# A WKV recurrence with routed experts on one core: block rows transposed on VectorE, strip sums on VectorE, two wide logits, one transfer for keys and decays

## The chip, the cores and the metric

One Trainium2 chip, one core of it, one launch. The metric is the device time of the program in microseconds (us); lower is better. All arithmetic that decides the result is float32.

## The reference

```python
def _attn_ref(r, k, v, w, u):                 # (4, 8, 768, 48) each, u (8, 48)
    for t in range(S):
        cur = einsum('bhd,bhe->bhde', u[None] * kt, vt)
        y[:, :, t] = einsum('bhd,bhde->bhe', rt, state + cur)
        state = wt[:, :, :, None] * state + einsum('bhd,bhe->bhde', kt, vt)

def _moe_ref(x, modality_id, w_gate, modality_bias, w1, w2):   # x (3072, 384)
    logits = x @ w_gate + modality_bias[modality_id]           # 8 experts
    e_idx = argmax(logits, axis=1)
    gate_w = softmax(logits)[arange(N), e_idx]
    for e in range(E):
        mask = e_idx == e
        h = maximum(x[mask] @ w1[e], 0.0)                      # 384 -> 1024
        out[mask] = gate_w[mask, None] * (h @ w2[e])           # 1024 -> 384
```

The rows of x are the attention's outputs with the heads side by side. Each row goes to one expert, its best.

## The kernel before, in words

The program has two stages. In the first, 24 units of 128 time steps (6 chunks in each of 4 sequences) run through a chunked form of the recurrence (`att_iter`). The loop is software-pipelined: in iteration `i` the decays and keys of unit `i+3`, the scan of unit `i+2`, the scores of unit `i+1` and the output of unit `i` are worked on. A unit's inputs are three parts of one tile of 1536 columns: r (0 to 512), k (512 to 1024) and the decays (1024 to 1536). `load` issues them on SP's queue, here in three transfers for units 4 to 23 (L913). The output of a unit (L455, PSUM tile `pY`) is added up into a row tile `xp` by VectorE (`x_rows`, L477). TensorE then transposes these rows, and `logits` (L504) multiplies them with the gate's weights, in six matmuls with 64 output rows each. Rows, gate weights and row numbers are scattered by expert into a table `xs` in HBM, one indirect transfer of GpSimd per unit (L711).

In the second stage seven blocks of rows run through an expert each: two of 512 rows, three of 384, one of 512, one of 416 (`WIDTH`; numbered 0 to 6 here). For block `q`:

- `blk_load(q)` (L732) brings its rows from `xs` into the tile `xl`, in one transfer on SP's queue, rows on partitions. It is issued one or more blocks ahead; block 0's is issued in iteration 20 of the first stage, block 1's waits for the scatters of the first ten units.
- `blk_t(q)` (L745) turns the rows: TensorE transposes them 64 rows at a time into four PSUM areas (L755; L758 for the odd 32 rows of block 6), ScalarE casts them to `xh` (L765), and VectorE takes the remainder to `xo` (L767). For block 0 this stands in the last iteration of the first stage, for block 2 ahead of the last tile of block 1's second half, for the others right behind the first half of the block before.
- `blk_up(q, g)` for g from 0 to 7 (L778) is the first half: nine matmuls each of 384 to 512 columns, with the weights split in two parts `wh` and `wl`. ScalarE evicts (`hh`, L782), VectorE takes the remainder (`hl`, L783).
- `blk_down(q, fs, js)` (L799) is the second half, one tile `j` of 128 rows after the other into `pY` and `pX` in turn, 24 matmuls each. `blk_out` (L817) scales it on ScalarE (`ot`, L822) and writes it with an indirect transfer of GpSimd (L823).
- The 32 odd rows of block 6 are a strip of their own: `strip_down` (L802) gives four partial sums on four groups of 32 partitions, ScalarE copies them (L810), and `strip_sum` (L813) adds them with a matmul against the matrix `fold`.

Between these calls the program runs small steps from a table `aux` (which block, which half, which step): the splitting of the next expert's weights (`w_split`, L270: a cast on ScalarE, a remainder on VectorE), the routing table, the scatters of later units, weight loads. Each engine carries out its instructions in the order of the program.

Of the kernel before, what the change touches and what calls it, by code (L numbers as in the profile page):

```python
# [70 lines left out]
def kernel(ctx: ExitStack, tc: tile.TileContext, rkw, vt, wf, cst, mid, wg, bias, w1, w2, out):  # L71
# [238 lines left out]
    def ok(n):  # L310
        return 0 <= n < NU
# [35 lines left out]
    def att_iter(i):  # L347
# [384 lines left out]
    def blk_load(q, at=None):  # L732
        at = q if at is None else at
        w = width(q) // P
        rest = width(q) % P
        xl = bp["m"].tile([P, BW // P, XW], F32, tag="xl", name=f"xl{q}", bufs=3)
        r = nc.sync.value_load(tab[0:1, 1, ds(at, 1)], min_val=0, max_val=DUMMY)
        ins = nc.sync.dma_start(out=xl[:, 0:w], in_=xs[ds(r, w * P), :].rearrange("(j p) c -> p j c", p=P))
        if q == 0:
            tc.add_to_no_dep_group("x0", ins.ins)  # L740
        if rest:
            nc.sync.dma_start(out=xl[0:rest, w], in_=xs[ds(r + w * P, rest), :])
        X["xl", q] = xl

    def blk_t(q):  # L745
        xl, w = X["xl", q], width(q)
        xh, xo = (bp["m"].tile([P, KC, BW], F32R, tag=t, name=f"{t}{q}", bufs=1) for t in ("xh", "xo"))
        pk, pu, nj = pt(f"x{q}_0", "pK", (P, 2, 512)), pt(f"x{q}_2", "pU"), w // P
        halves, m = [(0, KC - 1, (pk[:, 0], pk[:, 1])), (KC - 1, KC, (pu, pt(f"x{q}_3", "pS1" if q == WB else "pX")))], w % P
        for c0, c1, pp in halves:  # L750
            for c in range(c0, c1):
                for j in range(nj):
                    for pb, r in zip(pp, HALVES):
                        o = ((c - c0) * nj + j) * 64
                        nc.tensor.transpose(out=pb[:, o:o + 64], in_=xl[r, j, c * P:(c + 1) * P], identity=ident[r, r])  # L755
        o = 64 * nj
        for c in range(KC if m else 0):
            nc.tensor.transpose(out=pu[:, o + c * m:o + (c + 1) * m], in_=xl[0:m, nj, c * P:(c + 1) * P], identity=ident[0:m, 0:m])  # L758
        view = lambda t, c0, c1, h: t[:, c0:c1, 0:nj * P].rearrange("p c (j h b) -> p c j h b", h=2, b=64)[:, :, :, h]
        moves = [(lambda t, c0=c0, c1=c1, h=h: view(t, c0, c1, h), pb[:, 0:(c1 - c0) * nj * 64].rearrange("p (c j b) -> p c j b", c=c1 - c0, j=nj))  # L760
                 for c0, c1, pp in halves for h, pb in enumerate(pp)]
        if m:
            moves.append((lambda t: t[:, :, nj * P:w], pu[:, o:o + KC * m].rearrange("p (c b) -> p c b", c=KC)))
# [4 lines left out]
        X["x", q] = (xh, xo)  # L768

# [32 lines left out]
    def strip_down(q, j):  # L802
        r0, r1 = spans(width(q))[j]
        pp = pt(f"d{q}_{j}", "pK", (P, DM))
        for f in range(FC):
            i = f % (P // TAIL) * TAIL
            nc.tensor.matmul(out=pp[i:i + TAIL], lhsT=X["ht", q][:, f], rhs=raw[1][:, f],
                             start=(f < P // TAIL), stop=(f + P // TAIL >= FC), skip_group_check=True)
        st = bp["p"].tile([P, GW], F32, tag="wg", name=f"st{q}", bufs=2)[:, 0:DM]
        nc.scalar.copy(out=st, in_=pp)  # L810
        X["st", q] = st

    def strip_sum(q, j):  # L813
        X["y", q, j] = pt(f"s{q}_{j}", "pU", (P, DM))
        nc.tensor.matmul(out=X["y", q, j][0:TAIL], lhsT=fold, rhs=X["st", q], start=True, stop=True)

    def blk_out(q, js):  # L817
        xl = X["xl", q]
        for j in js:
            m = min(P, width(q) - j * P)  # L820
            ot = bp["p"].tile([P, DM], F32, tag="ot", name=f"ot{q}_{j}", bufs=4)
            nc.scalar.activation(out=ot[0:m], in_=X["y", q, j][0:m], func=AF.Copy, scale=xl[0:m, j, DM:DM + 1])  # L822
            ins = nc.gpsimd.indirect_dma_start(  # L823
                out=out[:, :], out_offset=bass.IndirectOffsetOnAxis(ap=xl[0:m, j, DM + 1:DM + 2].bitcast(I32), axis=0),
                in_=ot[0:m], in_offset=None, bounds_check=NT - 1, oob_is_err=False)
            if isinstance(q, int):
                rows_apart("out", ins)


    def half_load(q, at=None):  # L830
        at = q if at is None else at
        xl = bp["m"].tile([P, BW // P, XW], F32, tag="xl", name=f"xl{q}", bufs=3)
        r = nc.sync.value_load(tab[0:1, 1, ds(at, 1)], min_val=0, max_val=DUMMY)
        nc.sync.dma_start(out=xl[:, 0], in_=xs[ds(r, P), :])
        X["xl", q] = xl

    def half_t(q):
        pp = pt(f"x{q}", tag="pK", sh=(P, KC, P))
        for c in range(KC):
            nc.tensor.transpose(out=pp[:, c], in_=X["xl", q][:, 0, c * P:(c + 1) * P], identity=ident)  # L840
        X["x", q] = bp["p"].tile([P, KC, P], F32, tag="xq", name=f"xq{q}", bufs=1)
        nc.scalar.copy(out=X["x", q], in_=pp)
# [49 lines left out]
    for i in range(-2, NU):  # L892
# [93 lines left out]
    at(q1, "u", 6, part(nc.vector.tensor_reduce, out=fold, in_=ident.rearrange("p (i r) -> p r i", r=TAIL), axis=AX.X, op=ALU.add))  # L986
    fl = flags()
# [3 lines left out]
    for n, q in enumerate(seq):  # L991
# [10 lines left out]
        for j in range(nj):  # L1002
# [14 lines left out]
            if nxt is None and j == 1:  # L1017
                strip_sum(q, nj)
                blk_out(q, (nj,))
# [39 lines left out]
    def any_decay():  # L1059
# [40 lines left out]
        with tc.tile_pool(name="gmoe", bufs=1) as gp:  # L1100
# [48 lines left out]
def _layout(inp):  # L1149
# [15 lines left out]
    for hh in range(2):  # L1165
# [40 lines left out]
```

## Time and profile before

| what | value |
|---|---|
| median of 3 runs | 347.0 us (344.35 to 347.06) |
| profiled execution, own time | 345.26 us |
| its span, first to last instruction | 343.1 us |
| TensorE busy (matmul) | 329.9 us, 96% |
| VectorE, ScalarE, GpSimd busy | 225.7, 205.9, 156.4 us |
| granted TensorE clock, mean | 0.998 |

The span is 2.2 us shorter than the execution's own time. Matmul ends are modelled, so the busy share of TensorE is not its share of peak; the starts of its instructions are what the text reads. The first stage lasts to about 121 us of the span, the second from there to the end.

### The profile page before, as it was taken

The numbers are of one execution on the slowest core, as the hardware profiler recorded it, in microseconds if no ns is written. First come the engines' busy times: TensorE is split into PE (matmuls) and PEld (weight loads), VectorE is DVE, ScalarE is ACT, GpSimd is POOL, SyncE is SP. The second block draws the span as 40 slices with busy tenths as digits, with TensorE's granted clock in tenths as the row PEclk, the third lists the DMA queues.
The fourth block names the chain that finished last, engine by engine and source line by source line (L and its number), as shares of the span: only waits on it lengthen the run. The fifth ranks groups of instructions, "written<-read, shape, count | busy, mean of one in ns | idle before, by whom it ended". The sixth has DMA issues, their size and how long they took to land.

```text
span 343.1 us, 10458 instructions
## 1 busy us (share of the span) xinstructions
PE 329.9 (96%) x4064; PEld 303.2 (88%) x4064; DVE 225.7 (66%) x495; ACT 205.9 (60%) x524; POOL 156.4 (46%) x194
## 2 busy tenths in 40 slices
PE   7989999999999999999999999999999999999992
PEld 3788899989989987799889999999999988999972
DVE  7999999999999565871578369468067055615500
ACT  2577588687799874632467459658658645514320
POOL 5889999999996383075542201200200200121022
PEclk9999999999999999999999999999999999999999
DMA  7998988888983302248728300700700812210001
GB/s 230 400 288 244 293 272 262 272 254 243 313 249 111 94 3 97 90 151 255 247 88 249 121 2 0 254 23 0 278 24 3 303 36 91 107 50 18 1 26 59
DMA packets 24672, 52.32 MB, mean 153 GB/s; under 512 B 3045, under 2 KB 11045, under 8 KB 24612
## 3 DMA queue, kind: packets, MB, share of 16 engines
q1 hardware_dynamic: 21508, 42.08, 38.8%
q0 software_dynamic: 3104, 9.47, 7.5%
q8 instruction: 34, 0.56, 0.7%
q14 instruction: 26, 0.21, 0.2%
HBM read 55.43 MB, written 11.88 MB: 196 GB/s over the span
## 4 chain that ended last, share of the span: by engine, by line
issue 45%; PE 24%; POOL 12%; DMA 8%; DVE 3%; ACT 3%; POOLq 2%; SPq 0%; ACTq 0%
POOL out L823 6%; PE pY L455 5%; DMA in<-rkw 5%; PE pS L411 4%; POOL xs L711 4%; PE pY L444 4%; PE pR_x L317 3%; PE pU L429 2%; PE pR_x L507 2%; DMA xl<-xs 1%; POOLq L1016 1%; DMA v<-vt 1%; POOL wl L273 1%; PE pY_d L799 1%; ACT dV L352 1%
## 5 line engine op out<-in xcount | busy, mean ns | idle before, releaser
L823 POOL DMA_INDIRECT out<-ot,xl x25 | 26.1, 1046 | 141.2 <-ACT ot L822 139.9
L783 DVE SCALAR_TENSOR_TENSOR hl<-pS_u,hh 128x512 fp32r<-128x512 f32 (+2 forms) x56 | 34.6, 619 | 74.4 <-ACT hh L782 74.2
L778 PE MATMUL pS_u<-xh,wh 128*128 128x512 f32 (+2 forms) x168 | 61.8, 368 | 0.0
L778 PE MATMUL pS_u<-xh,wl 128*128 128x512 f32 (+2 forms) x168 | 61.3, 365 | 0.0
L782 ACT ACTIVATE hh<-pS_u 128x512 fp32r<-128x512 f32 (+2 forms) x56 | 30.3, 541 | 51.6 <-PE pS_u L778 51.5
L273 DVE TENSOR_TENSOR wl<-raw,wh 128x768 fp32r<-128x768 f32 x52 | 48.8, 963 | 3.6 <-ACT wh L272 3.3
L272 ACT CAST wh<-raw 128x768 fp32r<-128x768 f32 (+1 forms) x60 | 45.1, 799 | 0.0
L778 PE MATMUL pS_u<-xo,wh 128*128 128x512 f32 (+2 forms) x168 | 43.2, 365 | 0.0
L799 PE MATMUL pY_d<-wh,hh 128*128 128x384 f32 x112 | 38.5, 343 | 0.0
L799 PE MATMUL pY_d<-wl,hh 128*128 128x384 f32 x112 | 37.7, 337 | 0.0
L799 PE MATMUL pY_d<-wh,hl 128*128 128x384 f32 x112 | 37.7, 336 | 0.0
L711 POOL DMA_INDIRECT xs<-xp,posT x24 | 26.0, 1083 | 24.9 <-DVE posT L594 22.2
L331 DVE TENSOR_TENSOR_SCAN pX_s<-pw,pX_s 128x268 f32<-128x268 f32 x48 | 34.1, 710 | 0.8 <-POOL pw L278 0.4
L778 PEld LDWEIGHTS pS_u<-xh,wh 128*128 128x128 f32 x168 | 31.5, 188 | 3.2
L778 PEld LDWEIGHTS pS_u<-xh,wl 128*128 128x128 f32 x168 | 31.5, 188 | 3.1
L778 PEld LDWEIGHTS pS_u<-xo,wh 128*128 128x128 f32 x168 | 31.0, 188 | 3.4
L283 POOL TENSOR_TENSOR G<-in 128x512 f32<-128x512 f32 x24 | 31.4, 1310 | 4.3 <-DMA in<-rkw 4.3
L352 ACT ACTIVATE dV<-v,dT 128x48 f32<-128x48 f32 x120 | 29.7, 327 | 0.0
L413 DVE TENSOR_TENSOR A<-pS,cs 128x1024 f32<-128x1024 f32 x24 | 29.2, 1217 | 0.6 <-PE pS L411 0.6
L411 PE MATMUL pS<-R,K 64*128 64x128 f32 x384 | 27.0, 280 | 1.9 <-DVE A L413 1.4
L295 POOL TENSOR_TENSOR in<-in 128x512 f32<-128x512 f32 (+1 forms) x23 | 28.5, 1239 | 0.6
L455 PE MATMUL pY<-v,A 128*64 128x48 f32 x768 | 26.8, 222 | 0.7 <-issue 0.7
(331 smaller groups left out, 674.9 us busy)
## 6 DMA issues: line engine op xcount, KB each, us to landing
raw<-w SPq DMA_DIRECT2D x24, 768.0 KB
in<-rkw SPq DMA_DIRECT2D x66, 256.0 KB
v<-vt SPq DMA_DIRECT2D x24, 192.0 KB
wg<-wf SPq DMA_DIRECT2D x8, 576.0 KB
raw<-w SPq DMA_DIRECT2D x8, 384.0 KB
xl<-xs SPq DMA_DIRECT2D x3, 772.0 KB
xl<-xs SPq DMA_DIRECT2D x4, 579.0 KB
xs<-zt SPq DMA_DIRECT2D x8, 193.0 KB
```

Of the source, the lines that this page charges most:

```text
L272: nc.scalar.copy(out=wh[k][:, sl], in_=raw[k][:, sl])
L273: (eng or (nc.vector, nc.gpsimd)[k]).tensor_tensor(out=wl[k][:, sl], in0=raw[k][:, sl], in1=wh[k][:, sl].bitcast(F32), op=ALU.subtract)
L283: nc.gpsimd.tensor_tensor(out=G, in0=t[:, 0:512], in1=t[:, 512:1024], op=ALU.mult)
L331: nc.vector.tensor_tensor_scan(out=BE[:, ::step], data0=pp[:, ::step], data1=d1[:, ::step], initial=0.0, op0=ALU.mult, op1=ALU.max)
L352: nc.scalar.activation(out=dV[:, h], in_=v0[:, h], func=AF.Copy, scale=dT[:, h:h + 1])
L411: nc.tensor.matmul(out=pS[:, hh, p], lhsT=K[q, p], rhs=R[q, p], start=True, stop=True)
L455: nc.tensor.matmul(out=pY[q:q + 64, h * D:(h + 1) * D], lhsT=A[:, hh, p, q:q + 64], rhs=v[:, h * D:(h + 1) * D], start=(first(z) and h == ...
L711: rows_apart("xs", nc.gpsimd.indirect_dma_start(out=xs[:, :], out_offset=bass.IndirectOffsetOnAxis(ap=posT[:, n:n + 1], axis=0), in_=T["xb ...
L778: nc.tensor.matmul(out=pp, lhsT=wsrc[0][:, g, c * P:(c + 1) * P], rhs=xsrc[:, c, 0:w], start=(n == 0), stop=(n == 3 * KC - 1))
L783: nc.vector.scalar_tensor_tensor(out=hl, in0=pp, scalar=0.0, in1=hh.bitcast(F32), op0=ALU.max, op1=ALU.subtract)
L799: nc.tensor.matmul(out=X["y", q, j][0:r1 - r0], lhsT=hsrc[:, r0:r1], rhs=wsrc[1][:, f], start=(f == 0 and n == 0), stop=(f == FC - 1 and n ...
L823: ins = nc.gpsimd.indirect_dma_start(out=out[:, :], out_offset=bass.IndirectOffsetOnAxis(ap=xl[0:m, j, DM + 1:DM + 2].bitcast(I32), axis=0 ...
```

## The change

1. `blk_load` brings a block's rows in four transfers of 96 columns each, every one to 32 partitions (tile `xq`), and a fifth for gate weight and row number (tile `xg`). VectorE transposes squares of 32 by 32 (`blk_turn`, three instructions to a block) into an SBUF tile `xt`, from which ScalarE casts `xh` and VectorE takes `xo`, three instructions each. The rows of `w1` are stored in the order that this gives. No matmul of TensorE is left in `blk_t`. For block 0 two of the three turns stand behind iteration 22 and one behind the row sum of iteration 23.
2. The strip's four partial sums are added by one copy of 32 partitions on ScalarE and three additions on VectorE; the matmul with `fold` is gone.
3. The logits of units 22 and 23 are three matmuls of 128 output rows instead of six of 64.
4. Keys and decays of units 4 to 23 come in one transfer of 1024 columns.

```diff
         if ok(z - 1) and not far(z - 1):
             x_rows(z - 1)
+        if i == NU - 1:
+            blk_turn(0, (2,))
...
             nc.scalar.copy(out=T["xT", z - 2], in_=pS.rearrange("p h (a b) -> p h a b", a=KC))
-            blk_t(0)
+            blk_parts(0)
...
+        if i == NU - 2:
+            blk_turn(0, (0, 1))
...
     def logits(n):
+        if n >= NU - 2:
+            for c in range(KC):
+                nc.tensor.matmul(out=T["R"][:, n * E:(n + 1) * E], lhsT=T["xT", n][:, c], rhs=wgs[:, c],
+                                 start=(c == 0), stop=(c == KC - 1), skip_group_check=True)
+            return
...
     def blk_load(q, at=None):
...
-        xl = bp["m"].tile([P, BW // P, XW], F32, tag="xl", name=f"xl{q}", bufs=3)
-        ins = nc.sync.dma_start(out=xl[:, 0:w], in_=xs[ds(r, w * P), :].rearrange("(j p) c -> p j c", p=P))
+        xq, xg = x_tiles(q)
+        ins = [nc.sync.dma_start(out=xq[SQ * g:SQ * g + SQ, 0:w // SQ],
+                                 in_=xs[ds(r, w), QW * g:QW * g + QW].rearrange("(t p) c -> p t c", p=SQ)) for g in range(4)]
+        ins.append(nc.sync.dma_start(out=xg[:, 0:nj], in_=xs[ds(r, nj * P), DM:XW].rearrange("(j p) c -> p j c", p=P)))
...
+    def blk_turn(q, cs):
+        w = width(q)
+        if 0 in cs:
+            X["xt", q] = bp["m"].tile([P, KC, BW], F32, tag="xt", name=f"xt{q}", bufs=1)
+        for c in cs:
+            nc.vector.transpose(out=X["xt", q][:, c, 0:w], in_=X["xq", q][:, 0:w // SQ, SQ * c:SQ * c + SQ])
+
+    def blk_parts(q):
+        xt, w = X["xt", q], width(q)
+        xh, xo = X["x", q] = tuple(bp["m"].tile([P, KC, BW], F32R, tag=t, name=f"{t}{q}", bufs=1) for t in ("xh", "xo"))
+        for c in range(KC):
+            nc.scalar.copy(out=xh[:, c, 0:w], in_=xt[:, c, 0:w])
+        for c in range(KC):
+            nc.vector.tensor_tensor(out=xo[:, c, 0:w], in0=xt[:, c, 0:w], in1=xh[:, c, 0:w].bitcast(F32), op=ALU.subtract)
...
     def blk_t(q):
-                        nc.tensor.transpose(out=pb[:, o:o + 64], in_=xl[r, j, c * P:(c + 1) * P], identity=ident[r, r])
...
-            nc.tensor.transpose(out=pu[:, o + c * m:o + (c + 1) * m], in_=xl[0:m, nj, c * P:(c + 1) * P], identity=ident[0:m, 0:m])
...
-        for at, pp in moves:
-            nc.scalar.copy(out=at(xh), in_=pp)
-        for at, pp in moves:
-            nc.vector.tensor_tensor(out=at(xo), in0=pp, in1=at(xh).bitcast(F32), op=ALU.subtract)
+        blk_turn(q, range(KC))
+        blk_parts(q)
...
-        nc.scalar.copy(out=st, in_=pp)
-        X["st", q] = st
-
-    def strip_sum(q, j):
-        X["y", q, j] = pt(f"s{q}_{j}", "pU", (P, DM))
-        nc.tensor.matmul(out=X["y", q, j][0:TAIL], lhsT=fold, rhs=X["st", q], start=True, stop=True)
+        nc.scalar.copy(out=st, in_=pp[0:TAIL])
+        for i in range(TAIL, P, TAIL):
+            nc.vector.tensor_tensor(out=st, in0=pp[i:i + TAIL], in1=st, op=ALU.add)
+        X["y", q, j] = st
...
-            load(i + 2 + NIN, ((512, 1024), (1024, LIN), (0, 512)))
+            load(i + 2 + NIN, ((512, LIN), (0, 512)))
```

Three places of the order. First VectorE at the end of the first stage: `A` is the score mask of unit 23, `xp` the row sum of unit 22, `xt` the turned rows of block 0, `hl_0` its first remainder. Before:

```order
L413 TENSOR_TENSOR A_2692<-pS_2693,cs 128x1024
L477 TENSOR_TENSOR xp_1450<-pY_2717,dV_2680 128x384
L767 TENSOR_TENSOR xo_2768<-pK_x_0_2769,xh_2767 128x8x64 x2
L767 TENSOR_TENSOR xo_2768<-pU_x_2_2770,xh_2767 128x4x64
L767 TENSOR_TENSOR xo_2768<-pX_x_3_2771,xh_2767 128x4x64
L783 SCALAR_TENSOR_TENSOR hl_0_2898<-pS_u_0_2887,hh_0_2897 128x512
```

And in the changed kernel:

```order
L417 TENSOR_TENSOR A_2677<-pS_2678,cs 128x1024
L768 STREAM_TRANSPOSE xt_2735<-xq_2549 128x512 x2
L483 TENSOR_TENSOR xp_1437<-pY_2702,dV_2665 128x384
L768 STREAM_TRANSPOSE xt_2735<-xq_2549 128x512
L776 TENSOR_TENSOR xo_2757<-xt_2735,xh_2756 128x512 x3
L795 SCALAR_TENSOR_TENSOR hl_0_2857<-pS_u_0_2846,hh_0_2856 128x512
```

Two turns now stand ahead of the row sum of unit 22, so that sum waits in VectorE's queue for block 0's load.

Second ScalarE behind block 0's first half: `hh_7` is that half's last eviction, `xh` block 1's rows, `ex` the exponential of the routing, `wh` the next weights, `ot_0` and `ot_1` block 0's first results. Before:

```order
L782 ACTIVATE hh_7_3060<-pS_u_7_3050 128x512
L765 CAST xh_3072<-pK_x_0_3074 128x8x64 x2
L765 CAST xh_3072<-pU_x_2_3075 128x4x64
L765 CAST xh_3072<-pX_x_3_3076 128x4x64
L567 ACTIVATE ex<-pR_x 128x14x8
L272 CAST wh_68<-raw_66 128x768 x2
L822 ACTIVATE ot_0_3167<-pY_d_0_3109,xl_2569 128x384
L272 CAST wh_68<-raw_66 128x768 x2
L822 ACTIVATE ot_1_3239<-pX_d_1_3172,xl_2569 128x384
```

And in the changed kernel:

```order
L794 ACTIVATE hh_7_3018<-pS_u_7_3008 128x512
L774 CAST xh_3034<-xt_3030 128x512 x3
L578 ACTIVATE ex<-pR_x 128x14x8
L274 CAST wh_68<-raw_66 128x768 x2
L832 ACTIVATE ot_0_3100<-pY_d_0_3042,xg_2550 128x384
L274 CAST wh_68<-raw_66 128x768 x2
L832 ACTIVATE ot_1_3172<-pX_d_1_3105,xg_2550 128x384
```

The casts stand where they stood; they now read what VectorE has turned, and the first result is still queued behind them.

Third ScalarE at the end of the last block, with the strip (`st`, tile 3 of that block) between the results of its tiles 0, 1 and 2. In the changed kernel:

```order
L832 ACTIVATE ot_0_5096<-pY_d_0_5070,xg_4520 128x384
L822 COPY st_5110<-pK_d_3_5101 32x384
L832 ACTIVATE ot_3_5140<-st_5110,xg_4520 32x384
L832 ACTIVATE ot_1_5145<-pX_d_1_5115,xg_4520 128x384
L832 ACTIVATE ot_2_5175<-pY_d_2_5150,xg_4520 128x384
```

The order of ScalarE's steps is as before, with an `st` of 32 partitions instead of 128; what left is the matmul on TensorE between the tiles 1 and 2.

## Rows read from the trace of the kernel before

**Rows 1.** The page: busy time, share and instructions of each engine.

```profile
PE 329.9 (96%) x4064; PEld 303.2 (88%) x4064; DVE 225.7 (66%) x495; ACT 205.9 (60%) x524; POOL 156.4 (46%) x194
```

**Rows 2.** Timeline of TensorE (start, length, line) around the transposes of blocks 2, 5, 6.

```profile
188.65 0.34 PE L799 MATMUL pY_d<-wl,hh 128*128 128x384 f32 x1
188.82 0.33 PE L799 MATMUL pY_d<-wh,hl 128*128 128x384 f32 x1
...
190.07 0.33 PE L799 MATMUL pX_d<-wl,hh 128*128 128x384 f32 x1
...
258.81 0.69 PE L778 MATMUL pS_u<-xo,wh 128*128 128x384 f32 x3
...
260.62 0.36 PE L799 MATMUL pY_d<-wl,hh 128*128 128x384 f32 x1
...
289.05 0.86 PE L778 MATMUL pS_u<-xo,wh 128*128 128x512 f32 x3
...
291.13 0.34 PE L799 MATMUL pY_d<-wl,hh 128*128 128x384 f32 x1
```

**Rows 3.** Timeline of TensorE around the transposes of block 1.

```profile
139.25 0.39 PE L778 MATMUL pS_u<-xh,wl 128*128 128x512 f32 x1
139.48 0.86 PE L778 MATMUL pS_u<-xo,wh 128*128 128x512 f32 x3
140.95 0.71 PE L755 MATMUL pK_x<-cs,xl 64*128 64x64 f32 x16 [0.61 <-DMA xl<-xs]
...
142.12 0.34 PE L799 MATMUL pY_d<-wl,hh 128*128 128x384 f32 x1
```

**Rows 4.** Timeline of ScalarE behind block 0's first half, and one row of VectorE.

```profile
143.19 0.31 ACT L567 ACTIVATE ex<-pR_x 128x112 f32<-128x112 f32 x1
143.34 1.60 ACT L272 CAST wh<-raw 128x768 fp32r<-128x768 f32 x2
...
147.10 0.58 ACT L822 ACTIVATE ot<-pY_d,xl 128x384 f32<-128x384 f32 x1 [2.16 <-PE pY_d L799]
...
142.55 0.28 DVE L561 TENSOR_REDUCE ohs<-oh 128x8 bf16<-128x80 bf16 x1
```

**Rows 5.** Timeline at the end of the first stage: VectorE, then TensorE.

```profile
118.38 0.56 DVE L477 TENSOR_TENSOR xp<-pY,dV 128x384 f32<-128x384 f32 x1 [1.42 <-ACT wh L272]
...
119.25 0.88 PE L444 MATMUL pY<-SPb,R 128*64 128x96 f32 x16
```

**Rows 6.** Block 0's load on SP's queue, and block 1's in the chain.

```profile
110.65 0.40 SPq L738 DMA_DIRECT2D xl<-xs  x1
...
135.95 4.96 DMA xl<-xs
```

**Rows 7.** DMA views of 3.0:3.5, 3.5:4.0 and 18.0:18.5; q1: packets, MB, share.

```profile
q1 hardware_dynamic: 102, 0.20, 102.8%
...
DMA packets 195, 0.15 MB, mean 307 GB/s; under 512 B 30, under 2 KB 150, under 8 KB 195
...
q1 hardware_dynamic: 195, 0.15, 95.8%
...
DMA packets 244, 0.16 MB, mean 329 GB/s; under 512 B 147, under 2 KB 209, under 8 KB 244
...
q1 hardware_dynamic: 244, 0.16, 112.2%
```

**Rows 8.** The page's groups: form, count, busy, mean ns of one, idle before.

```profile
L783 DVE SCALAR_TENSOR_TENSOR hl<-pS_u,hh 128x512 fp32r<-128x512 f32 (+2 forms) x56 | 34.6, 619 | 74.4 <-ACT hh L782 74.2
L413 DVE TENSOR_TENSOR A<-pS,cs 128x1024 f32<-128x1024 f32 x24 | 29.2, 1217 | 0.6 <-PE pS L411 0.6
```

**Rows 9.** Timeline of the last block: TensorE around the strip's sum, then GpSimd.

```profile
331.53 0.33 PE L799 MATMUL pX_d<-wh,hl 128*128 128x384 f32 x1
...
332.83 0.33 PE L799 MATMUL pY_d<-wl,hh 128*128 128x384 f32 x1
...
337.92 0.98 POOL L823 DMA_INDIRECT out<-ot,xl  x1 [2.22 <-ACT ot L822]
```

More of the change, by code (lines that the diff above doesn't have):

```diff
@@ L36 @@
 BT = WIDTH[-1]
+SQ = 32
+QW = DM // 4
 TAIL = BT % P
@@ L733, in blk_load @@
         at = q if at is None else at
-        w = width(q) // P
-        rest = width(q) % P
-        xl = bp["m"].tile([P, BW // P, XW], F32, tag="xl", name=f"xl{q}", bufs=3)
+        w = width(q)
+        nj, rest = divmod(w, P)
+        xq, xg = x_tiles(q)
         r = nc.sync.value_load(tab[0:1, 1, ds(at, 1)], min_val=0, max_val=DUMMY)
-        ins = nc.sync.dma_start(out=xl[:, 0:w], in_=xs[ds(r, w * P), :].rearrange("(j p) c -> p j c", p=P))
+        ins = [nc.sync.dma_start(out=xq[SQ * g:SQ * g + SQ, 0:w // SQ],
+                                 in_=xs[ds(r, w), QW * g:QW * g + QW].rearrange("(t p) c -> p t c", p=SQ)) for g in range(4)]
@@ L739, in blk_load @@
+        ins.append(nc.sync.dma_start(out=xg[:, 0:nj], in_=xs[ds(r, nj * P), DM:XW].rearrange("(j p) c -> p j c", p=P)))
         if q == 0:
-            tc.add_to_no_dep_group("x0", ins.ins)
+            for i in ins:
+                tc.add_to_no_dep_group("x0", i.ins)
         if rest:
-            nc.sync.dma_start(out=xl[0:rest, w], in_=xs[ds(r + w * P, rest), :])
-        X["xl", q] = xl
-    def blk_t(q):
[L746 to L754, printed above, removed]
-                        nc.tensor.transpose(out=pb[:, o:o + 64], in_=xl[r, j, c * P:(c + 1) * P], identity=ident[r, r])
-        o = 64 * nj
-        for c in range(KC if m else 0):
-            nc.tensor.transpose(out=pu[:, o + c * m:o + (c + 1) * m], in_=xl[0:m, nj, c * P:(c + 1) * P], identity=ident[0:m, 0:m])
[L759 to L763, printed above, removed]
-        for at, pp in moves:
-            nc.scalar.copy(out=at(xh), in_=pp)
-        for at, pp in moves:
-            nc.vector.tensor_tensor(out=at(xo), in0=pp, in1=at(xh).bitcast(F32), op=ALU.subtract)
-        X["x", q] = (xh, xo)
@@ new lines, in blk_load, with x_tiles @@
+            nc.sync.dma_start(out=xg[0:rest, nj], in_=xs[ds(r + nj * P, rest), DM:XW])
+    def x_tiles(q):
+        xq = X["xq", q] = bp["m"].tile([P, BW // SQ, QW], F32, tag="xq", name=f"xq{q}", bufs=2)
+        xg = X["xg", q] = bp["m"].tile([P, BW // P, 2], F32, tag="xg", name=f"xg{q}", bufs=3)
+        return xq, xg
+    def blk_turn(q, cs):
+        w = width(q)
+        if 0 in cs:
+            X["xt", q] = bp["m"].tile([P, KC, BW], F32, tag="xt", name=f"xt{q}", bufs=1)
+        for c in cs:
+            nc.vector.transpose(out=X["xt", q][:, c, 0:w], in_=X["xq", q][:, 0:w // SQ, SQ * c:SQ * c + SQ])
@@ L831, in half_load @@
         at = q if at is None else at
-        xl = bp["m"].tile([P, BW // P, XW], F32, tag="xl", name=f"xl{q}", bufs=3)
+        xq, xg = x_tiles(q)
         r = nc.sync.value_load(tab[0:1, 1, ds(at, 1)], min_val=0, max_val=DUMMY)
-        nc.sync.dma_start(out=xl[:, 0], in_=xs[ds(r, P), :])
-        X["xl", q] = xl
+        for c in range(KC):
+            nc.sync.dma_start(out=xq.rearrange("p t c -> p (t c)")[:, c * P:(c + 1) * P].rearrange("p (g i) -> p g i", i=SQ),
+                              in_=xs[ds(r, P), 0:DM].rearrange("p (g k i) -> p g k i", g=4, k=KC)[:, :, c])
+        nc.sync.dma_start(out=xg[:, 0], in_=xs[ds(r, P), DM:XW])
     def half_t(q):
@@ L839, in half_t @@
         for c in range(KC):
-            nc.tensor.transpose(out=pp[:, c], in_=X["xl", q][:, 0, c * P:(c + 1) * P], identity=ident)
+            nc.tensor.transpose(out=pp[:, c], in_=X["xq", q].rearrange("p t c -> p (t c)")[:, c * P:(c + 1) * P], identity=ident)
         X["x", q] = bp["p"].tile([P, KC, P], F32, tag="xq", name=f"xq{q}", bufs=1)
@@ L1017 @@
             if nxt is None and j == 1:
-                strip_sum(q, nj)
                 blk_out(q, (nj,))
@@ L1104, in any_decay @@
             wgf = mk("gwg", [P, KC, E])
-            nc.sync.dma_start(out=wgf, in_=wg.rearrange("(c p) e -> p c e", p=P))
+            for g in range(4):
+                nc.sync.dma_start(out=wgf[SQ * g:SQ * g + SQ], in_=wg[QW * g:QW * g + QW].rearrange("(c i) e -> i c e", i=SQ))
             with tc.For_i(0, E, 1) as e:
@@ L1110, in any_decay @@
                 with tc.For_i(0, NU, 1) as n:
-                    nc.sync.dma_start(out=xl, in_=xd[ds(n * P, P), :])
+                    for c in range(KC):
+                        nc.sync.dma_start(out=xl[:, c * P:(c + 1) * P].rearrange("p (g i) -> p g i", i=SQ),
+                                          in_=xd[ds(n * P, P), :].rearrange("p (g k i) -> p g k i", g=4, k=KC)[:, :, c])
                     px, pl, ph, py = pt("gx", "pX"), pt("gl", "pR"), pt("gh", "pS0"), pt("gy", "pY")
```

17 lines of the change are left out of this document (7 added, 10 removed).

## The prediction

> **What bounds the kernel now.** I read the page first. TensorE is busy 96% of the span, the next engine 66% [rows 1], and the granted clock is full throughout, so nothing is to be had from the clock. Then I followed TensorE's own timeline through the second stage, by the starts of its instructions, because the ends are modelled. Inside a half the starts are evenly spaced: 0.17 us for a matmul of 384 columns [rows 2], 0.23 us for one of 512 [rows 3]. TensorE is only off this beat where something else stands in its queue: at each block's transposes and at the strip's sum. So in this stage a microsecond taken out of TensorE's queue is a microsecond off the end, as long as what stood beside it is not late. The end confirms this: the last result goes out when GpSimd has waited 2.22 us for ScalarE [rows 9], which follows the last matmul.
>
> There is one true wait of TensorE in the stage: 0.61 us at block 1, for the load of its rows [rows 3]. The loads of blocks 0 and 1 are the two that are issued late, since they wait for scatters; those of the others are issued most of a block ahead. So I looked at the loads next (SP's timeline, the chain, the DMA view), because the change makes them slower.
>
> **The transposes of blocks 2 to 6 (the main gain).** The cost of a block's transposes is the distance between the last matmul ahead and the second one behind, less the beats that belong to matmuls. I take the second one because the first still loads its weights behind the transposes.
> - Block 2, 18 transposes: 190.07 - 188.82 = 1.25, less two beats of 0.17: 0.91 us. Blocks 3 and 4 have the same 18, so 3 x 0.91 = 2.73.
> - Block 5, 24 of them: 260.62 - 258.81 = 1.81, less four beats of 0.17: 1.13.
> - Block 6, 18 and 3 of the odd rows: 291.13 - 289.05 = 2.08, less three beats of 0.23 and one of 0.17: 1.22 [rows 2, 3].
> Together 5.1 us. In their place VectorE gets three turns per block. None is in the trace. The nearest row is `hl` with as many columns, 0.62 us; the other end is 1.22 us, what VectorE takes for 1024 columns [rows 8]. I take 0.62, since the form is one pass over 512 columns; it can't be nothing, each being an instruction of full width. The casts and remainders stay and become three of each. What hides them is the second half of the block before, 12.5 us for three tiles. Tightest is ScalarE's queue: casts of `xh`, four of `wh`, then the first result, which must be out before the third tile can use the same PSUM area, 48 beats or 8.4 us behind the start. At 0.62 a turn this leaves over a microsecond. For block 2 the turns come later, ahead of the last tile, and their cover is that tile.
>
> **Block 1.** Distance 142.12 - 139.48 = 2.64, less three beats of 0.23 and one of 0.17: 1.78 us, the wait for the load included [rows 3]. Not all comes home. The routing matmuls behind the first twelve matmuls need `ohs`, which VectorE ends at 142.83 [rows 4]; without the transposes TensorE is there at 140.17 + 2.1 = 142.3. So 0.5 us turn into a new wait, and 1.28 remain, if the load isn't too late (below).
>
> **Block 0.** Its transposes end where TensorE starts L444, at 119.25. That matmul overwrites `pY`, so it needs the row sum of unit 22, which VectorE ends at 118.94 [rows 5]. Of the transposes only 0.25 us can be gained; the rest becomes a wait for that sum. Two turns now stand ahead of that sum. VectorE was idle for 1.42 us there, from 116.96 [rows 5]; two turns of 0.62 are done at 118.2 and just fit. At 1.22 each they end at 119.4 and L444 starts at 120.0: a loss of 0.8.
>
> **The load in small packets.** One transfer of 512 packets of 1.5 KB becomes four of 512 packets of 384 bytes: 128 to each of the 16 DMA engines instead of 32. From 3.0 to 3.5 us nearly all packets have 2 KB: 102.8% of 16 x 0.5 us over 102 packets is 81 ns each. From 3.5 to 4.0 us, 45 of these leave 4.0 us for 150 smaller ones, most of 512 bytes: 27 ns each. From 18.0 to 18.5 us, 35 of 2 KB and 62 between leave 147 under 512 bytes with 16 to 30 ns, depending on what the 62 cost (61 or 27 ns) [rows 7]. I take p = 27 ns for 384 bytes; the ends are 16 and, if a packet costs the same whatever its size, 81. Block 1's load took 4.96 us [rows 6], of which 32 packets of 61 ns (by size from 81) are 1.95; the fixed part is 3.0. The issues of the four transfers, 0.4 us each [rows 6], run beside the data. So a load lands 3.0 + 0.128 p (p in ns) behind its first issue: 6.5 us.
> - Block 0: 110.65 + 6.5 = 117.1, some 0.15 behind VectorE's idle start. With turns, sum and hand-over (1.24 + 0.56 + 0.05) L444 starts at 119.0 at the earliest. Net: 3.74 - 0.128 p, at most 0.25.
> - Block 1: 135.95 + 6.5 = 142.4. ScalarE then needs three turns (1.86), the last cast (0.6), the exponential (0.31), two casts of weights (1.60) and the result (0.58) [rows 4]: 147.4. TensorE needs the PSUM area at 140.17 + 8.4 + 0.5 = 149.1. Cover is 1.7 us, gone from p = 40 ns; beyond it costs 0.128 ns for ns.
>
> The Trainium skill (DMA: Bandwidth & Descriptors, section Specifications) sets 512 bytes as the smallest transfer at line rate, with a read-modify-write below. The rows of 18.0 to 18.5 us don't show that: packets under 512 bytes cost no more there than those of 512 [rows 7]. By the rule p would be higher than 27; what that does is the third rival.
>
> For the turn the skill has a price (VectorE: DVE Perf Modes, the three transpose paths): 311 ns for 128 by 128 in bf16. Four of these, as an estimate, are 1.24 us, the upper end above. No trace here shows it; by it the sum would be that of the second rival.
>
> **The strip.** 332.83 - 331.53 = 1.30, less two beats: 0.96 us off TensorE's queue, with 5.3 us of work still to come behind it [rows 9]. VectorE's three additions (under 0.6 each by the rows of VectorE) run beside tile 1 and have nothing behind them. Since the strip's own result goes out earlier, GpSimd is free for the last one.
>
> **Logits and merged load.** The two wide logits have half the matmuls with twice the weight columns: I count nothing, with 0.3 us either way. The merged transfer carries the same bytes to a unit that is used two iterations later; decays came second before and land with the keys now. At 81 ns per 2 KB, 128 packets more on 16 engines are 0.65 us, once, if an early unit waits; an issue of 0.4 us on SP's queue is the most that it can save there. Later GpSimd and TensorE set the pace, so zero.
>
> **Sum.** 5.1 + 1.28 + 0.25 + 0.96 = 7.6 us. From the profiled execution's 345.26 that gives 337.7; from the median of the runs, 347.0, it gives 339.4. I forecast the middle, 338.5 (base 346.1).
>
> **Rivals.**
> 1. The freed time is eaten by a wait that takes its place: the first result of a block, behind turns, casts and weights on ScalarE, holds the third tile. For it: that queue order [rows 4] and a gap of a microsecond only. Against: by the rows it fits in every block. Then only the strip pays: 345.1.
> 2. A turn costs 1.22 us. Block 0 loses 0.8 instead of winning 0.25; in block 5 ScalarE's queue is late by about 1.0, in block 6 by 0.3. 7.6 - 2.3 = 5.3: 340.8. For it is only the price on a page; against it, that rows of 512 columns all lie near 0.62 [rows 8].
> 3. Packets of 384 bytes cost double those of 512, p = 54 ns. Block 0: 3.74 - 6.91 = -3.2. Block 1: 1.28 - 1.8 = -0.5. Sum 5.1 + 0.96 - 3.7 = 2.4: 343.7. Against: the rows of 18.0 us.
> 4. Slower: the loads of blocks 0 and 1 land so late that VectorE, waiting in order for the rows, holds the row sum and with it TensorE, and ScalarE holds block 0's first result. The total is 11.1 + 5.1 - 0.256 p, nothing at p = 63 ns. If packets cost the same whatever their size, 81 ns, it is -4.5: 350.6. For it: SP's queue gets four times the packets at the two places without slack. Against: 27 ns at 512 bytes.
>
> **Chances.** The forecast 0.64; rival 1 0.06; rival 2 0.13; rival 3 0.11; rival 4 0.06. A measurement of this kernel can tell about 1% (3.5 us) from no change. Faster by over 1%: forecast and rival 2, and half of rival 3 (its 343.7 lies 0.7% below the base, but 0.95% below the median): 0.82. Within 1%: rival 1 and the rest: 0.12. Slower: 0.06. The range, 336 to 344, holds the forecast from either base with the logits' bounds and a faster packet, and rivals 2 and 3; it leaves out rivals 1 and 4.
>
> **What would show it.** Right: TensorE goes from the first to the second half of blocks 3 to 6 without leaving its beat; turns of 0.6 us; a wait of half a microsecond at the routing matmuls; L444 released by the row sum; the last block without a gap between tiles 1 and 2. Wrong: VectorE idle for the load ahead of its turns in block 0 by more than 0.2 us, a wait of TensorE at the third tile of a block for ScalarE's result, turns of over a microsecond, or a first stage whose length changes by more than half a microsecond.

## The result and the profile after

The changed kernel takes 342.45 us in the median of 20 runs (340.23 to 345.13), the kernel before 345.57 (344.35 to 349.41). The ratio is 0.9892, 95% interval 0.9871 to 0.9914: a gain of 1.1%, at the edge of the 1% that the prediction set for "faster". Direction and range hold, but of the 7.6 us that it counted only some 3 to 4 came: 338.5 was 4 us too low. The profiled execution (345.13 us, span 343.3) is the slowest of the 20, so it has to be read stage by stage. Ratios compare runs in the fast state; two of one_load's six runs (341.54 and 345.02 us) were slow ones and are not in its ratio.

The page's engine row, against [rows 1], and its row of the granted clock by slices:

```profile
PE 326.3 (95%) x3903; PEld 302.6 (88%) x3903; DVE 239.1 (70%) x510; ACT 206.5 (60%) x516; POOL 157.9 (46%) x194
...
PEclk9999999898999999989999999999999999999999
```

161 matmuls are gone, VectorE has 13 us more, and TensorE's share did not rise. The clock, which the kernel before had in full until its end, has three dips. The starts of TensorE's matmuls cut each program into stretches (us; the last cut is the modelled end of the last matmul; two of the experiments stand beside):

| stretch | before | after | ex_first | merged_again |
|---|---|---|---|---|
| up to block 0's first matmul | 121.32 | 125.52 | 123.68 | 121.07 |
| block 0, first half | 20.52 | 18.94 | 18.94 | 18.94 |
| block 0, second half | 17.78 | 22.14 | 18.13 | 17.35 |
| block 1, first half | 16.80 | 17.00 | 18.70 | 16.80 |
| block 1, second half, to block 5's end | 131.37 | 125.79 | 125.80 | 125.78 |
| block 6, first half | 13.91 | 13.80 | 13.81 | 13.84 |
| block 6, second half (the strip) | 15.28 | 14.30 | 14.28 | 14.28 |
| behind the last matmul | 6.09 | 5.84 | 5.86 | 5.68 |

What was to be gained was gained: 1.58 us at block 1's transposes, 5.58 at those of blocks 2 to 6, 0.98 at the strip. Two stretches gave it back: block 0's second half (+4.36) and, in this execution, the first stage (+4.20).

**Block 0's second half.** The timeline of the kernel after, TensorE, then ScalarE, then VectorE (start, length, engine, line; in brackets the idle time ahead and what ended it):

```profile
146.37 0.34 PE L811 MATMUL pY_d<-wh,hl 128*128 128x384 f32 x1
149.79 0.21 PE L587 MATMUL pR_x<-oh,cs 128*128 128x112 bf16 x1 [3.08 <-ACT ex L578]
...
150.82 0.51 PE L811 MATMUL pY_d<-wh,hl 128*128 128x384 f32 x1
...
147.77 1.80 ACT L774 CAST xh<-xt 128x512 fp32r<-128x512 f32 x3 [2.52 <-DVE xt L768]
149.48 0.26 ACT L578 ACTIVATE ex<-pR_x 128x112 f32<-128x112 f32 x1
...
146.65 0.28 DVE L569 TENSOR_TENSOR pR_x<-pR_x,mx 128x112 f32<-128x112 f32 x1
146.84 0.28 DVE L572 TENSOR_REDUCE ohs<-oh 128x8 bf16<-128x80 bf16 x1
147.04 1.89 DVE L768 STREAM_TRANSPOSE xt<-xq 128x512 f32<-128x512 f32 x3
```

The routing matmuls wait 3.08 us, and not for `ohs`, which is done at 147.12, but for the exponential `ex`, which reads the PSUM tile that they write. Its input, the tile that VectorE wrote at L569, was ready at 146.93. It stands in ScalarE's queue behind the three casts `xh`, and these now wait for VectorE's turns. In the kernel before the casts read PSUM as soon as TensorE had transposed, and `ex` ended at 143.50 [rows 4], before TensorE got there, without a wait:

```profile
144.07 0.22 PE L576 MATMUL pR_x<-oh,cs 128*128 128x112 bf16 x1
```

Behind the wait of the changed kernel the clock falls, as the windows show (PEclk is the column behind POOL):

```profile
145.00:150.00 5.00, 1.92 (x15) 1.69 (x15) 4.64 (x10) 2.48 (x6) 0.00 (x0) 1.00 0.02 1
150.00:155.00 5.00, 5.00 (x35) 5.00 (x32) 3.03 (x9) 1.95 (x4) 1.97 (x2) 0.66 0.16 58
155.00:160.00 5.00, 5.00 (x30) 5.00 (x30) 4.04 (x17) 1.87 (x3) 3.64 (x4) 1.00 0.39 143
...
56.00:58.00 2.00, 1.20 (x26) 1.07 (x27) 1.97 (x4) 0.12 (x1) 2.00 (x3) 1.00 0.83 223
58.00:62.00 4.00, 4.00 (x80) 3.93 (x76) 2.24 (x5) 2.70 (x11) 4.00 (x6) 0.58 0.72 233
```

From 150 to 155 us the mean is 0.66, that is mostly the level of 1.2 GHz: a matmul of 384 columns comes every 0.32 us instead of 0.17 until 154. The last two rows show the same in the first stage: TensorE idles 0.8 of two microseconds, and the next four run at 0.58.

**Block 0's entry**, VectorE and then TensorE, against [rows 5]:

```profile
119.00 0.56 DVE L483 TENSOR_TENSOR xp<-pY,dV 128x384 f32<-128x384 f32 x1 [1.59 <-PE pY L459]
...
121.32 1.29 DVE L768 STREAM_TRANSPOSE xt<-xq 128x512 f32<-128x512 f32 x2
122.82 0.56 DVE L483 TENSOR_TENSOR xp<-pY,dV 128x384 f32<-128x384 f32 x1 [0.20 <-ACT wh L274]
...
121.56 1.12 PE L459 MATMUL pY<-v,A 128*64 128x48 f32 x32
123.44 0.80 PE L448 MATMUL pY<-SPb,R 128*64 128x96 f32 x14 [0.43 <-DVE xp L483]
124.47 1.12 PE L459 MATMUL pY<-v,A 128*64 128x48 f32 x32
```

The two turns run without a wait for the load, the row sum follows, and it releases L448 (L444 before), as forecast. The distance between the last two units, by the starts of their output matmuls (L459), is 2.91 us instead of 3.16 (120.28 - 117.12 at L455 before): the 0.25 of the prediction. It is 2.91 in merged_again and 2.95 in ex_first too.

**The small packets and the turns.** The DMA view of 140 to 147 us, block 1's load, and the turns by form (count, busy, mean ns):

```profile
DMA packets 2640, 0.79 MB, mean 113 GB/s; under 512 B 2640, under 2 KB 2640, under 8 KB 2640
...
q1 hardware_dynamic: 2640, 0.79, 57.5%
```

```profile
L768 DVE STREAM_TRANSPOSE xt<-xq 128x512 f32<-128x512 f32 x9 | 5.8, 683 | 0.0
L768 DVE STREAM_TRANSPOSE xt<-xq 128x384 f32<-128x384 f32 x9 | 4.5, 548 | 0.0
```

57.5% of 16 x 7 us over 2640 packets is 24 ns each, but that is a mean over two kinds. Packet by packet the trace has 2048 of 384 bytes, the rows, with 28.6 ns each, and 592 of 8 or 4 bytes, 512 of them for `xg`, with about 10 ns. A turn of 512 columns takes 0.68 us, one of 384 columns 0.55.

**Blocks 5 and 6 and the strip**, TensorE's timeline, against [rows 2, 9]:

```profile
262.82 0.69 PE L790 MATMUL pS_u<-xo,wh 128*128 128x384 f32 x3
263.35 0.34 PE L811 MATMUL pY_d<-wh,hh 128*128 128x384 f32 x1
263.52 0.34 PE L811 MATMUL pY_d<-wl,hh 128*128 128x384 f32 x1
...
291.92 0.86 PE L790 MATMUL pS_u<-xo,wh 128*128 128x512 f32 x3
292.62 0.33 PE L811 MATMUL pY_d<-wh,hh 128*128 128x384 f32 x1
...
332.99 0.34 PE L811 MATMUL pX_d<-wh,hl 128*128 128x384 f32 x1
333.16 0.34 PE L811 MATMUL pY_d<-wh,hh 128*128 128x384 f32 x1
```

From half to half and from tile to tile TensorE now keeps its beat; nothing of the transposes or of the strip's sum is left in its queue.

### The profile page after: what moved, and what is told of

It is laid out like the page before. It is cut to its first block, busy times and chain, and to the rows that moved or that the text cites. A ratio compares the mean times of both kernels' runs of the same rounds, so it can differ in the third digit from the quotient of the medians.

```text
span 343.3 us, 10172 instructions
## 1 busy us (share of the span) xinstructions
PE 326.3 (95%) x3903; PEld 302.6 (88%) x3903; DVE 239.1 (70%) x510; ACT 206.5 (60%) x516; POOL 157.9 (46%) x194
## 4 chain that ended last, share of the span: by engine, by line
issue 35%; PE 35%; POOL 5%; ACT 4%; DVE 3%; POOLq 2%; DMA 2%; SPq 1%; ACTq 0%; DVEq 0%
PE pS_u L790 10%; POOL out L833 5%; PE pY L459 4%; PE pS L415 4%; PE pY L448 3%; PE pR_x L319 2%; PE pX_d L811 2%; PE pY_d L811 2%; PE pU L433 2%; DMA wg<-wf 2%; POOLq L1026 1%; PE pR_x L518 1%; ACT dV L354 1%; DVE wl L275 1%; ACT pU L436 1%
## 5 line engine op out<-in xcount | busy, mean ns | idle before, releaser
L833 POOL DMA_INDIRECT out<-ot,xg x25 | 26.8, 1072 | 133.9 <-ACT ot L832 128.4
L811 PE MATMUL pY_d<-wh,hl 128*128 128x384 f32 x112 | 38.4, 343 | 0.0
L459 PE MATMUL pY<-v,A 128*64 128x48 f32 x768 | 28.2, 229 | 0.0
```

The source lines that it names most:

```text
L459: nc.tensor.matmul(out=pY[q:q + 64, h * D:(h + 1) * D], lhsT=A[:, hh, p, q:q + 64], rhs=v[:, h * D:(h + 1) * D], start=(first(z) and h == ...
L811: nc.tensor.matmul(out=X["y", q, j][0:r1 - r0], lhsT=hsrc[:, r0:r1], rhs=wsrc[1][:, f], start=(f == 0 and n == 0), stop=(f == FC - 1 and n ...
L833: ins = nc.gpsimd.indirect_dma_start(out=out[:, :], out_offset=bass.IndirectOffsetOnAxis(ap=xg[0:m, j, 1:2].bitcast(I32), axis=0), in_=ot[ ...
```

## Experiments on the wait at block 1

**ex_first**: the exponential ahead of the casts.

```
-    at(q0, "u", FC - 1, part(next, ra1), part(next, ra1), part(blk_raw, q1, 1))
-    at(q0, "d", 0, part(route_x, 1))
+    at(q0, "u", FC - 1, part(next, ra1), part(next, ra1), part(route_x, 1), part(blk_raw, q1, 1))
```

> Theory A: the gain was eaten at block 1, where the exponential on ScalarE stands behind three casts that wait for VectorE's turns, so that TensorE waits 3.08 us at the routing matmuls and then runs some us at a lower clock. With the exponential ahead of the casts it ends 0.3 us behind its input: the wait falls from 3.08 to 0.4 to 0.7 us, the stretch from block 0's first second-half matmul to block 1's first first-half matmul falls from 22.14 to 18.2 to 18.6 us, the granted clock of that stretch is 1.00, and the median falls by 2.5 (the wait alone) to 4 us (wait and clock), from 342.45 to 338.5 to 340. Rival B: the gain was eaten in the first stage, and TensorE would have waited at block 1 for the casts or the first result anyway: the wait moves from the routing matmuls to the third tile, and the median falls by less than 1 us.

Measured: 339.25 us, ratio 0.9815 (0.9778 to 0.9852). Its timeline, TensorE, then ScalarE:

```profile
144.53 0.34 PE L811 MATMUL pY_d<-wh,hl 128*128 128x384 f32 x1
145.50 0.21 PE L587 MATMUL pR_x<-oh,cs 128*128 128x112 bf16 x1 [0.63 <-ACT ex L578]
...
160.57 0.34 PE L811 MATMUL pX_d<-wh,hl 128*128 128x384 f32 x1
...
145.19 0.27 ACT L578 ACTIVATE ex<-pR_x 128x112 f32<-128x112 f32 x1 [1.77 <-DVE pR_x L569]
145.93 1.80 ACT L774 CAST xh<-xt 128x512 fp32r<-128x512 f32 x3 [0.48 <-DVE xt L768]
...
156.79 0.58 ACT L832 ACTIVATE ot<-pY_d,xg 128x384 f32<-128x384 f32 x1 [3.58 <-PE pY_d L811]
164.90 0.58 ACT L832 ACTIVATE ot<-pX_d,xg 128x384 f32<-128x384 f32 x1 [7.52 <-PE pS_u L790]
```

The wait is 0.63 us, the stretch 18.13 (a little under the 18.2 to 18.6 expected), the clock in it full: theory A. So the misplaced exponential cost 22.14 - 18.13 = 4.0 us, of which 2.45 are the wait; the other 1.56 go with the 3.4 us at the lower clock. The median fell by 3.2 only. The profiled execution, at 341.10 us one of the slower ones, has a second wait: ScalarE's last result of block 0 started at 164.90, though its last matmul had started at 160.57. TensorE waited for what stands behind it, and block 1's first half took 18.70 us instead of 16.80.

**ex_ohs_first**, and the same program again as **merged_again**: `ohs` and its three predecessors a step earlier as well.

```
     at(q0, "u", 5, part(next, ra1))
-    at(q0, "u", FC - 1, part(next, ra1), part(next, ra1), part(blk_raw, q1, 1))
-    at(q0, "d", 0, part(route_x, 1))
+    at(q0, "u", 6, part(next, ra1), part(next, ra1))
+    at(q0, "u", FC - 1, part(route_x, 1), part(blk_raw, q1, 1))
```

> As ex_first, and the last four routing instructions of VectorE (the scan, the one-hot, the subtraction and the sum `ohs`) one step earlier, ahead of the last remainder `hl` instead of behind it. Theory A: the last 0.5 us of wait at the routing matmuls are for `ohs` and go too: the stretch is 17.7 to 18.0 us and the median 0.3 to 0.6 us below that of ex_first. Rival: the last remainder `hl` then comes 0.9 us late and TensorE waits for it at the second-half matmuls instead, so that the time is that of ex_first within 0.3 us or above it.

> The kernel of ex_ohs_first once more (338.25 us, with ScalarE's last result of block 0 late by 4.4 us). If that stall is chance of one execution, block 1's first half takes 16.8 us this time and the median is near 336.5 to 337; if it belongs to this program, the half takes about 19 us again and the median is 338 to 338.5.

Measured: 338.25 us, ratio 0.9774 (0.9746 to 0.9803), and the second time 336.25, ratio 0.9769 (0.9721 to 0.9818). In both the stretch is 17.35 us, 0.78 less than in ex_first, where 17.7 to 18.0 had been expected. The 0.63 us of wait went too; in ex_first it was still a wait for the exponential, which itself stood 1.77 us for L569, one of the four steps moved here. The first time ScalarE's result was late again (block 1's first half 19.02 us); the second time it was not (16.80), though two of the six runs took 339.4 and 339.5 us. TensorE and ScalarE of merged_again:

```profile
141.92 0.34 PE L811 MATMUL pY_d<-wh,hl 128*128 128x384 f32 x1
142.10 0.22 PE L587 MATMUL pR_x<-oh,cs 128*128 128x112 bf16 x1
...
157.56 0.58 ACT L832 ACTIVATE ot<-pX_d,xg 128x384 f32<-128x384 f32 x1 [3.58 <-PE pX_d L811]
```

One program gave both, so the order of the instructions alone does not decide that lateness. What ScalarE waited for, no view shows. In both late profiles SP's issues of zero rows beside it were drawn out (six in 9.97 us in ex_first, four in 7.23 in ex_ohs_first, three in 2.92 in merged_again); whether that is the cause is not shown.

**late_pads**: the eight transfers of zero rows behind block 2's weights.

```
-        at(q1, "u", e // 2, part(pad_rows, e))
+        at(q1, "u", FC - 1, part(pad_rows, e))
```

> The kernel of ex_ohs_first with the eight transfers that write zero rows issued behind block 2's weights instead of among them. In ex_first and ex_ohs_first ScalarE's last result of block 0 came 4.1 and 4.4 us behind its matmul, so that TensorE waited in block 1's first half, which took 18.7 and 19.0 us instead of 16.8. Theory P (that stall comes from the burst of these transfers with the scatters beside them): block 1's first half takes 16.8 to 17.2 us and the median falls by 1.5 to 2 us, to 336.5. Rival: the stall has another cause; it stays, and the median is within 0.5 us of 338.25.

Measured: 340.75 us, ratio 0.9900 (0.9869 to 0.9932): slower than what it started from. Block 1's first half took 16.80 us, but so it did in merged_again without the edit, which decides nothing about theory P. The edit made a wait of its own: block 2's load stands behind the zero rows, its casts are late, and the clock falls behind the wait (TensorE, then a window with PEclk 0.57):

```profile
190.67 0.34 PE L811 MATMUL pX_d<-wh,hl 128*128 128x384 f32 x1
193.96 0.44 PE L790 MATMUL pS_u<-xh,wh 128*128 128x384 f32 x1 [2.96 <-ACT xh L774]
```

```profile
194.00:198.00 4.00, 4.00 (x13) 3.84 (x14) 2.08 (x5) 2.25 (x5) 0.98 (x1) 0.57 0.98 240
```

## Experiments on the merged load and the first stage

**three_loads** undoes the merged load in the changed kernel, **before_merged** makes it in the kernel before, **ex_ohs_three_loads** (and again **three_again**) undoes it in ex_ohs_first, **one_load** puts all three parts of a unit into one transfer there.

```
-            load(i + 2 + NIN, ((512, LIN), (0, 512)))
+            load(i + 2 + NIN, ((512, 1024), (1024, LIN), (0, 512)))
```

```
-            load(i + 2 + NIN, ((512, LIN), (0, 512)))
+            load(i + 2 + NIN, ((0, LIN),))
```

> The changed kernel with a unit's keys and decays in two transfers again, all else as changed. Theory M (the merged load makes the first stage longer, by late data and the clock that falls behind the waits): the first matmul of block 0 comes at 121.3 to 123 us instead of 125.5, the mean granted clock over the runs rises from 0.990 to 0.993 or more, and the median falls by 1.5 to 4 us. Rival N (the 4.2 us of the profiled execution are that of one execution, whatever the load's form): the median stays within 1 us of 342.45, and the mean clocks spread over 0.983 to 0.997 as before.

Measured: 342.31 us against 342.45 with the merged load.

> The kernel before with the merged load alone. Theory M: the median rises by 1.5 to 4 us, and the clocks of the runs spread down to 0.985. Rival N: within 1 us of the kernel before, clocks as there.

Measured: ratio 1.0012 (0.9987 to 1.0037) to the kernel before.

> The kernel of ex_ohs_first with keys and decays in two transfers. Theory M (the merged load makes the first stage longer): the median falls by 1 us or more below 338.25. Rival N (the merged load is worth nothing either way, and the first stage varies by some us from execution to execution): within 1 us of 338.25.

> The kernel of ex_ohs_three_loads once more (it measured 336.26 us), beside merged_again in the same call. Theory M (the merged load costs the first stage 1 us or more): the difference of the medians, after taking off any stall of ScalarE in block 1's first half that the profile of either shows, is 1 us or more. Rival N (it costs nothing; in the undisturbed executions unit 22 ends at 117.1 us with either form): the difference without the stall is under 1 us.

Measured: 336.26 us, ratio 0.9746 (0.9709 to 0.9783); this is 2.0 below ex_ohs_first, which looks like theory M. But 2.2 us of the profiled execution of ex_ohs_first are ScalarE's late result. Beside each other on one chip three_again took 336.21 (ratio 0.9752, 0.9717 to 0.9786) and merged_again 336.25, with block 0's first matmul at 121.27 and 121.07.

> The kernel of ex_ohs_first with a unit's keys, decays and receptances in a single transfer: the merged load taken one step further. Theory M: the first stage gets longer again by about what the merged load cost, and the median lies 1 us or more above merged_again (block 1's first half taken alike). Rival N: within 1 us of it.

Measured: ratio 0.9765 (0.9704 to 0.9826), that of merged_again, and block 0's first matmul at 121.68. The median of all six runs is 338.16 us (335.61 to 345.02), so for this form the runs leave more open than for the others.

Rival N holds to within about 1 us: no pair of runs tells the forms apart. But all four pairs lean the same way, with the merged load slower by 0.1 to 0.3% (0.9892 against 0.9880, 1.0012 against 1, 0.9774 against 0.9746, 0.9769 against 0.9752), so that a cost of up to 1 us is not excluded. The 4.2 us of the profiled execution are for the most part that execution's: programs with the same first stage reached block 0 at 125.52 (the changed kernel), 123.68 (ex_first), 121.88 (ex_ohs_first) and 121.07 (merged_again), and before_merged did at 123.16. On the way the clock fell twice in the changed kernel's profile, once in ex_first's, and not in the other three.

## Experiments on the other steps

**strip_pe**: the strip's sum back on TensorE, in ex_ohs_first.

```
-        st = bp["p"].tile([P, GW], F32, tag="wg", name=f"st{q}", bufs=2)[0:TAIL, 0:DM]
-        nc.scalar.copy(out=st, in_=pp[0:TAIL])
-        for i in range(TAIL, P, TAIL):
-            nc.vector.tensor_tensor(out=st, in0=pp[i:i + TAIL], in1=st, op=ALU.add)
+        st = bp["p"].tile([P, GW], F32, tag="wg", name=f"st{q}", bufs=2)[:, 0:DM]
+        nc.scalar.copy(out=st, in_=pp)
...
+        nc.tensor.matmul(out=X["y", q, j][0:TAIL], lhsT=fold, rhs=X["st", q], start=True, stop=True)
```

> The kernel of ex_ohs_first with the strip's partial sums added by TensorE again, as in the kernel before. Theory by the prediction's step: TensorE's queue gets 0.96 us longer between tiles 1 and 2 of the last block. Theory by the trace of the changed kernel: 1.1 us on TensorE and 0.3 us behind it, since GpSimd then has the strip's result to send first: 1.4 us. Rival: VectorE's three additions and their hand-over were not free, and the strip costs the same on either engine, within 0.3 us.

Measured: 338.0 us, ratio 0.9790 (0.9757 to 0.9822), against 336.25 of merged_again; the strip is 1.0 us of these 1.75; the profile also has a first stage 1.8 us longer, which is not the strip's. Its timeline of TensorE:

```profile
325.99 0.33 PE L811 MATMUL pX_d<-wh,hl 128*128 128x384 f32 x1
326.25 0.83 PE L827 MATMUL pU_s<-st,fold 128*32 128x384 f32 x2
327.01 0.44 PE L811 MATMUL pY_d<-wh,hh 128*128 128x384 f32 x1
327.29 0.33 PE L811 MATMUL pY_d<-wl,hh 128*128 128x384 f32 x1
```

327.29 - 325.99 is 1.30, less two beats 0.95: the prediction's 0.96. The half takes 15.28 us instead of 14.28. The 0.3 us behind TensorE did not show (5.80 and 5.68 us behind the last matmul).

**turns_twice**: each turn of blocks 2 to 6 done twice, in ex_ohs_first.

```
-        for c in cs:
+        for c in sorted([*cs, *(cs if q not in (0, 1) else ())]):
```

> The kernel of ex_ohs_first, with every turn of blocks 2 to 6 done twice on VectorE (the same result). Theory A (the turns of these blocks lie beside TensorE's work with over a microsecond to spare, as the prediction's cover says): TensorE keeps its beat into each second half, the median stays within 0.5 us of ex_ohs_first (338.25). Rival (the prediction's second rival, which works with turns of this cost: ScalarE's queue is late by 1.0 us in block 5 and 0.3 us in block 6): TensorE waits at the third tile of these two blocks, and the median rises by 1.0 to 1.5 us.

Measured: 340.0 us, ratio 0.9859 (0.9821 to 0.9898). The rival holds: in the second halves of blocks 4 and 5, which cover the turns of blocks 5 and 6, TensorE waits at the third tile for ScalarE's first result.

```profile
264.82 0.45 PE L811 MATMUL pY_d<-wh,hh 128*128 128x384 f32 x1 [0.97 <-ACT ot L832]
...
294.90 0.45 PE L811 MATMUL pY_d<-wh,hh 128*128 128x384 f32 x1 [0.54 <-ACT ot L832]
```

0.97 and 0.54 us, where the prediction's second rival had worked out 1.0 and 0.3. The stretches of blocks 2 to 6 together grew by 2.8 us against merged_again, more than the 1.0 to 1.5 expected: the second halves of blocks 2 and 3, where no lateness was expected, take 0.33 longer each. Three turns more are 2.05 us at 512 columns; less the wait of 0.97 this leaves 1.1 us that TensorE had to spare for block 5, the prediction's cover of over a microsecond.

**narrow_logits**: the logits of the last two units in halves of 64 rows, in ex_ohs_three_loads.

```
-        if n >= NU - 2:
-            for c in range(KC):
-                nc.tensor.matmul(out=T["R"][:, n * E:(n + 1) * E], lhsT=T["xT", n][:, c], rhs=wgs[:, c],
...
```

> The kernel of ex_ohs_three_loads with the logits of the last two units in two halves of 64 rows again. The prediction's step (nothing, with 0.3 us either way): block 0's first half takes 18.9 us within 0.3, as with wide logits, and the median stays within 1 us of three_again. Rival (the wide form is worth its half of the matmuls): that half is 0.4 us longer or more.

Measured: 335.91 us, ratio 0.9728 (0.9696 to 0.9760); block 0's first half takes 18.85 us instead of 18.94. The wide form is worth nothing that shows.

## Why the prediction was right, and where it was wrong

- **The transposes of blocks 2 to 6**: right, 5.58 us for 5.1. The half microsecond more lies in the second halves behind the transposes, which are 0.1 to 0.3 us shorter each. The turn was sized 0.62 and took 0.68 us at 512 columns and 0.55 at 384. The Trainium skill (VectorE: DVE Perf Modes, the three transpose paths) had led to an estimate of 1.24 us; the trace disagrees, with little more than half of it.
- **The load in small packets**: right in what it decided, neither block waits for it. A packet of 384 bytes took 28.6 ns, near the 27 that was taken. Of the rows behind that figure, those of 18.0 to 18.5 us were misread: the packets under 512 bytes there have 4 and 64 bytes and take 10 to 11 ns in the trace, so they say nothing of 384 bytes. Those of 512 bytes at 3.5 to 4.0 us were the right ones to ask; they took 28.9. The load was sized too long: from its first issue to its last packet block 1's took 5.3 us (140.13 to 145.39) against 4.5 before (135.95 to 140.45), 0.8 us more where 1.5 were counted. The Trainium skill (DMA: Bandwidth & Descriptors, section Specifications) asks for 512 bytes; a packet of 384 bytes takes no longer than one of 512 here, though for fewer bytes.
- **Block 0** (0.25), **the strip** (0.96) and **the logits** (0): right, measured 0.25, 0.98, and nothing. For **the merged load** (0) the runs show a cost between nothing and 1 us.
- **Block 1**: this step failed, at the sentence that 0.5 us turn into a new wait. It released the routing matmuls by `ohs` alone and left out `ex`. The prediction had all that it needed: its list of ScalarE's work had the exponential behind the last cast [rows 4], but asked of that list only when the first result comes out. By its own numbers the load lands at 142.4, three turns and the last cast and the exponential end at 145.2, and TensorE is there at 142.3: a wait of 2.9 us. Measured were 3.08. That the two are so close is in part luck: in the run the load was not what came last, the turns started at 147.04 right behind `ohs` in VectorE's queue.
- **"Nothing is to be had from the clock"**: the second fault. The wait of 3 us cost more than itself, since the matmuls behind it ran at the lower level: 1.56 us.

Stage by stage the profiles give 5.58 + 0.98 + 0.25 + 1.58 - 4.36 = 4.0 us instead of 7.6; the whole difference is block 1, -2.78 instead of +1.28, with half a microsecond more at blocks 2 to 6 on the other side. From the 345.57 of 20 runs (the prediction's base was half a microsecond higher) this is 341.5; measured were 342.45. The other 0.9 us are not placed; the first stage, which varied by 4 us between executions, could hold them. That the result lies in the range is luck in part too: the range reached to 344 for slower turns and costlier packets, and what came was neither.

With both removed (merged_again) the program takes 336.25 us, ratio 0.9769 to the kernel before: with ScalarE's and VectorE's queues put in order the change is worth 8 us by the ratio, 8.7 by the medians (336.25 against 344.94 beside it), and the order that it came with hid more than half of that. The kernel before was not run in the new order; its trace has no wait at the routing matmuls to take away. The nearest rival was the first, a wait on ScalarE's queue in place of the freed time; it named the first result and the third tile; what came was the exponential and the routing matmuls, at one block.

## What to carry to other kernels

When a producer moves to another engine, the instruction that consumes it may stay where it was in its queue and still begin to block: go through everything that stands behind it on that engine, and ask of each who waits for it, not only of the one that looks latest. A wait of 3 us on TensorE cost 1.56 us more by the clock behind it, so such a wait is not priced by its length alone. Before a stage's change in a single profile is explained, look at how much that stage varies between executions of the same program.

## What the runs showed that was not expected

- After TensorE's waits of 3.08 us (the changed kernel), 3.1 (three_loads) and 2.96 us (late_pads) the granted clock went to 1.2 GHz for three to four microseconds each time. After 0.63 us (ex_first) and 1.23 us (ex_ohs_first, block 1) it stayed full; in the first stage of the changed kernel it fell twice behind idle times of 1.19 us.
- The lateness of ScalarE by 4 us in the profiles of ex_first and ex_ohs_first, while the second of these programs ran without it as merged_again. Whether transfers or something else held it is open.
